# A second 7-for-8 level, in part, for the first FFN products of the last two blocks

## Chip, cores, metric

One core of a Trainium2 chip runs the whole program. The metric is device microseconds of one launch, the median of several runs. All arithmetic is in float32; the FFN weights arrive as 64-bit floats and are rounded by the kernel first.

## What is computed

```python
# attention: batch 8, heads 12, seq 448, head_dim 64
q_n, k_n = rmsnorm(q, g_q), rmsnorm(k, g_k)
attn = softmax(q_n @ k_n.T / 8)
o = attn @ v                                   # (8, 12, 448, 64)
x = o.transpose(0, 2, 1, 3).reshape(3584, 768)
# bilinear FFN: w_a, w_b are 768 x 1536, w_out is 1536 x 768
out = ((x @ w_a) * (x @ w_b)) @ w_out
```

## The kernel before, in words

**Order of the work.** Nothing is issued in the order of the source. Every step is a call `op(engine, us, key, emit, reads, writes, ...)` of a planner (`Plan`). It simulates the engines with the given costs, respects the named reads and writes and the number of buffers of each tag, and where several steps could start on an engine takes the one with the lowest key:

```python
t = min(at.values()) + (0.2 if e == "PE" else 0.05)      # line 128: how far it looks ahead
n = min((n for n in at if at[n] <= t), key=lambda n: (ops[n][2], n))
```

A step of another engine can start `LAG` = 0.1 us after what it needs. The result is one fixed order for each engine, written out at the end; the hardware then follows it, each engine strictly in its order, with semaphores where data or buffers pass between engines. Attention has keys below 24, FFN products keys from 10,000 up: matrix work of the FFN fills what attention leaves free.

**Attention.** The 96 (batch, head) pairs are taken four at a time, `p` from 0 to 23. `loads` (line 424) brings q, k, v; `normalize` squares (ACT), reduces (DVE) and takes the power -1/2 (POOL); `transposes` turns q and k on TensorE; `scores` (line 507), the exponentials on ACT, `values` (line 527) and the sums over keys follow for seven key tiles; `put_out` (line 623) copies the result into two of nine buffers of the tag `x`, and `divide` multiplies by the inverse sums. Three `p` make a batch, two batches a block; there are four blocks (`beta` 0 to 3, called blocks 1 to 4 in words).

**First FFN products.** Block `beta` holds its transposed x as four quarters B11, B21, B12, B22 (two batches by two halves of the 768 features, each 128 partitions x 3 chunks x 448 tokens). `combine` (line 653) makes three more sums T2, T3, T4 on DVE, so that a block takes seven of the nine `x` buffers. `quarter_products` (line 987) then runs, for each of 6 row groups `m` and each of the two weights, the seven products of a Strassen-Winograd scheme (seven products of half size in place of eight): each product is three matmuls of 128x128 weights by 448 tokens that add up over the three chunks. The seven weight factors were made at the start, written to DRAM (`kept`) and are streamed back by `stream` (line 406) into two buffers of the tag `st`. Each product of the second weight is multiplied into the first in `hT`, part of it on POOL.

**Last FFN products.** `last_product` (line 687) multiplies `hT` by w_out in seven products again, for tiles `t` of 128 tokens (three in an even block, four in an odd one). In blocks 3 and 4 `TWICE` (line 309) has pairs of tiles go through `inner_products` (line 859): a second level of seven products, of 128x192, with extra weight factors streamed from `kept_t` by `stream_inner` (line 846). `inner_factors` makes these during block 2.

**The order around the change.** `ffn(beta)` (line 668) is `quarter_products` for all `m`, then `last_product`. With seven of nine `x` buffers held by a block, attention can put out only one batch more until the block's first products are done; so in the trace `put_out` pauses during the first products of blocks 1, 2 and 3. The results of `p` = 21 to 23 are put out after the first products of block 3 (1137 to 1158 us), and then its last products and all of block 4 follow. `hT` has one buffer, so first products of a block wait for the last products of the block before.

## Time and profile before

| | |
|---|---|
| median of 3 runs | 1546.28 us (1545.95 to 1547.28) |
| profiled execution, first to last instruction | 1544.2 us |
| difference of the two, launch and end around the span | 2.1 us |
| TensorE clock granted | 0.999 of full |
| PE busy | 1503.3 us, 97% |
| DVE busy | 824.4 us, 53% |
| ACT busy | 401.9 us, 26% |
| POOL busy | 314.6 us, 20% |
| first products of one block alone on PE (block 4) | 189.43 us, 504 matmul instructions |

"Span" is one profiled execution; the runs are timed without a profile. A float32 matmul of the program shows as two matmul instructions (passes): the program has 12 x 7 x 3 = 252 matmuls for the first products of a block, and the chain shows 504 instructions. Each matmul instruction has a weight load (PEld) beside it. [...]what one costs in a stream is the distance from start to start. In the names of groups `pq` is a bank of the first products, `po` of the last products, `a` to `h` of `inner_products`, `sc`, `o` and `su` are attention.

### The profile page before, as it was taken

How to read it: one execution, taken by the hardware profiler on the slowest of the kernel's cores; microseconds unless marked ns; L12 is line 12 of the kernel's file. 1: busy time of each engine (PE TensorE's matmuls, PEld its weight loads, DVE VectorE, ACT ScalarE, POOL GpSimd, SP SyncE). 2: the span in 40 equal slices, each digit the busy share in tenths (PEclk: the TensorE clock that was granted, in tenths of full speed). 3: DMA queues.
4: the chain of work that ended last, by engine and by line, in shares of the span. 5: the costliest groups of instructions: out<-in, count | busy, mean ns of one | idle time of the engine just before them, and what ended most of it. 6: DMA issues, size and time to landing. Idle time of an engine off the chain costs nothing.

```text
span 1544.2 us, 18272 instructions
## 1 busy us (share of the span) xinstructions
PE 1503.3 (97%) x7068; PEld 832.2 (54%) x7068; DVE 824.4 (53%) x1215; ACT 401.9 (26%) x658; POOL 314.6 (20%) x166
## 2 busy tenths in 40 slices
PE   8988999999999999999999999999999999999998
PEld 5554345555454555555445455555546865555898
DVE  5877869888786412222587553222237622222785
ACT  6767661111567200000455500000041000000000
POOL 3417442211345200011244300000111001100100
PEclk9999999999999999999999999999999999999999
DMA  9897444544545542212345456222126752212354
GB/s 265 241 255 218 98 109 178 204 178 158 158 111 133 150 153 72 107 72 102 94 114 147 111 172 187 91 77 102 72 78 224 225 193 72 107 72 102 119 184 120
DMA packets 130019, 217.12 MB, mean 141 GB/s; under 512 B 57988, under 2 KB 108420, under 8 KB 120196
## 3 DMA queue, kind: packets, MB, share of 16 engines
q1 hardware_dynamic: 101860, 162.38, 35.9%
q10 hardware_dynamic: 28064, 53.48, 10.0%
q8 instruction: 58, 0.95, 0.3%
q14 instruction: 37, 0.30, 0.1%
HBM read 171.44 MB, written 44.21 MB: 140 GB/s over the span
## 4 chain that ended last, share of the span: by engine, by line
PE 83%; DMA 7%; ACT 3%; DVE 3%; issue 1%; POOL 1%; SPq 1%; ACTq 0%; DVEq 0%; POOLq 0%
PE pq L1003 49%; PE po L726 14%; PE sc L515 5%; PE o L537 5%; PE g L901 2%; PE a L901 2%; ACT ET L521 2%; DMA q_sb<-in_q_dram 2%; PE pt L494 2%; DMA kept_o<-st 2%; PE b L901 1%; PE su L573 1%; PE d L901 1%; PE e L901 1%; DMA k_sb<-in_k_dram 1%
## 5 line engine op out<-in xcount | busy, mean ns | idle before, releaser
L1003 PE MATMUL pq<-x,st 128*128 128x448 f32 x2016 | 763.4, 540 | 0.0
L1003 PEld LDWEIGHTS pq<-x,st 128*128 128x128 f32 x2016 | 381.2, 190 | 378.4 <-issue 370.5
L521 ACT ACTIVATE ET<-sc,ms 128x448 f32<-128x448 f32 x336 | 192.0, 635 | 92.6 <-PE sc L515 64.9
L515 PE MATMUL sc<-qkT 64*64 64x448 f32 x1344 | 177.0, 544 | 18.6 <-ACT ET L521 10.7
L537 PE MATMUL o<-ET,v_sb 64*64 64x448 f32 x1344 | 186.9, 546 | 8.0 <-ACT ET L521 7.3
L464 POOL TENSOR_TENSOR ms<-ms,expo 128x14 f32<-128x14 f32 x48 | 145.4, 3032 | 190.4 <-DVE ms L462 189.6
L1051 POOL TENSOR_TENSOR hT<-hT,t 128x448 f32<-128x448 f32 x24 | 28.5, 1186 | 743.6 <-DVE t L1049 741.3
L726 PE MATMUL po<-st,hT 128*128 128x384 f32 x432 | 142.9, 487 | 0.0
L726 PEld LDWEIGHTS po<-st,hT 128*128 128x128 f32 x432 | 81.3, 190 | 58.5 <-issue 3.4
L515 PEld LDWEIGHTS sc<-qkT 64*64 64x64 f32 x1344 | 58.7, 132 | 94.7 <-issue 32.8
L551 POOL TENSOR_TENSOR sum<-sum,ET 128x896 f32<-128x896 f32 x38 | 81.6, 2147 | 137.6 <-ACT ET L521 106.1
L1025 ACT COPY hT<-pq 128x448 f32<-128x448 f32 x24 | 12.8, 532 | 371.3 <-PE pq L1003 371.3
L537 PEld LDWEIGHTS o<-ET,v_sb 64*64 64x64 f32 x1344 | 60.3, 132 | 88.5 <-ACT ET L521 42.3
L726 PE MATMUL po<-st,fin 128*128 128x384 f32 x240 | 81.8, 491 | 0.0
L551 DVE TENSOR_TENSOR sum<-sum,ET 128x896 f32<-128x896 f32 x57 | 62.8, 1101 | 27.0 <-POOL sum L551 22.7
L1063 POOL TENSOR_TENSOR hT<-hT,t 128x448 f32<-128x448 f32 x48 | 59.0, 1231 | 53.4 <-DVE t L1060 45.2
L458 DVE TENSOR_REDUCE ms<-sq 128x14 f32<-128x896 f32 x48 | 51.8, 1079 | 28.9 <-ACT sq L456 28.9
L1056 DVE TENSOR_TENSOR hT<-U,pq 128x448 f32<-128x448 f32 x48 | 29.8, 621 | 66.2 <-PE pq L1003 66.2
L726 PEld LDWEIGHTS po<-st,fin 128*128 128x128 f32 x240 | 44.6, 190 | 35.8 <-issue 7.8
L1060 DVE TENSOR_TENSOR t<-U,pq 128x448 f32<-128x448 f32 x48 | 29.7, 619 | 58.7 <-PE pq L1003 56.6
L1028 ACT COPY t<-pq 128x448 f32<-128x448 f32 x24 | 12.8, 533 | 176.0 <-PE pq L1003 176.0
L746 DVE TENSOR_TENSOR o_sb<-fin,po 128x384 f32<-128x384 f32 x32 | 17.7, 554 | 69.2 <-PE po L726 61.5
(117 smaller groups left out, 1372.5 us busy)
## 6 DMA issues: line engine op xcount, KB each, us to landing
st<-kept SPq DMA_DIRECT2D x36, 1344.0 KB
st<-kept_o SPq DMA_DIRECT2D x28, 1152.0 KB
kept<-st ACTq DMA_DIRECT2D x12, 1344.0 KB
ti<-kept_t SPq DMA_DIRECT2D x56, 288.0 KB
q_sb<-in_q_dram SPq DMA_DIRECT2D x48, 224.0 KB
k_sb<-in_k_dram SPq DMA_DIRECT2D x48, 224.0 KB
v_sb<-in_v_dram SPq DMA_DIRECT2D x48, 224.0 KB
rec<-inv SPq DMA_DIRECT2D x48, 224.0 KB
```

Source lines behind the costliest of these rows:

```text
L458: op("DVE", 1.1, key, lambda: nc.vector.tensor_reduce(rs[p][:, s], xs["sq", nm, p], AX, ALU.add), [sq], [f"{ms}/{nm}"])
L464: lambda: nc.gpsimd.tensor_tensor(msf(), msf(), expo[:, 0:2 * NT * (b - a)], ALU.pow), [], names)
L494: nc.tensor.transpose(t[:, j * P:(j + 1) * P], x[:, j].rearrange("p h d -> p (h d)"), ident)
L515: nc.tensor.matmul(t[low_high[w], e, 0:S], lhsT=qkTs[p][low_high[e], 1, j * P + w * D:j * P + (w + 1) * D], rhs=qkTs[p][low_high[e], 0, w ...
L521: nc.scalar.activation(E[:, e], scs[p, j][:, e, 0:S], AF.Exp, scale=rs[p][:, 1, 2 * j + e:2 * j + e + 1])
L537: nc.tensor.matmul(os_[p][low_high[e], w, 0:S], lhsT=xs["v", p][low_high[w], e, j * D:(j + 1) * D], rhs=ETs[p, j][low_high[w], e], start=( ...
L551: two[e].tensor_tensor(sums[p], sums[p] if j > 1 else ETs[p, 0], ETs[p, j], ALU.add)
L726: nc.tensor.matmul(held["po"][:, 0:HALF], lhsT=a[0]()[:, c], rhs=sts[beta, 12 + place_of[f]][:, c], start=(c == 0), stop=(c == MH - 1))
L901: nc.tensor.matmul(held[bank], lhsT=x()[:, c], rhs=y(c), start=(start and c == 0), stop=(stop and c == MI - 1), skip_group_check=True)
L1003: nc.tensor.matmul(banks[bank][:, 0:S], lhsT=sts[at][:, f, c * P:(c + 1) * P], rhs=quads[x][:, c], start=(start and c == 0), stop=(stop an ...
L1056: take("DVE", 0.68, lambda bank=bank, i=i, n=n: V.tensor_tensor(C(i, n), held["U"], PS(bank), ALU.add), [f"p{ident_}.{bank}", U], [hp[i]])
L1063: lambda i=i, n=n, nm=nm: two[TIMES].tensor_tensor(C(i, n), C(i, n), held[nm], ALU.mult), [t], [hp[i]],
```

## The change

1. Blocks 3 and 4 (`DEEP`) no longer use `quarter_products`. `deep_products` takes the two weights together: for each `m` and each of the seven factors `f` it forms a two-by-two product (two weights by two chunks of the sum, two halves of 224 tokens) with one more seven-for-eight level over chunks 1 and 2 of 3, and plainly adds the third chunk. A step (m, f) has 11 matmuls of 224 tokens; its part of the work before was 12 of that size. There are 42 steps in a block.
2. The extra weight factors are made during the first products of block 2 (`PREP`) by `deep_factors` (5 DVE steps on 896 elements and 5 DRAM writes of 448 KB for each m) and streamed back with the old ones, three transfers of 640 KB together for each step, into quarters of the two `st` buffers. The token sums (4 DVE steps for each of 7 quarters) sit in buffers of attention (`ET`, `sum`, `rec`, `qn`).
3. The products leave PSUM into seven buffers F (tags `q`, `k`, `v`, `sq`), are combined there by DVE (`wide`), and multiplied by POOL into `hT` (`times`).
4. In the plan, attention from `p` = 15 on is loaded after the first products of block 2, all attention ends before the deep products of block 3, and T2 and T4 of block 3 are made after it, in `qkT` buffers, so that nine `x` buffers do.
5. In blocks 3 and 4 the last product f = 0 is a plain one (`TWICE` without 0), split in halves over the sum, the first of which need only the first three `m`.

The diff, cut to its core:

```diff
-        TWICE = {NB - 2: (0, 1, 2, 3, 4, 5, 6), NB - 1: (0, 1, 2, 3, 4, 5, 6)}
+        TWICE = {NB - 2: (1, 2, 3, 4, 5, 6), NB - 1: (1, 2, 3, 4, 5, 6)}
         MAKE = 1
         ONCE = NB - 2
+        DEEP, PREP = (NB - 2, NB - 1), NB - 3
+        HELD = 2 * HC * (PREP + 1) + HC * (XS - 7) // 2
...
-            op("SP", 0.8 if nm != "k" else 1.4, p - (1.8 if nm == "v" else 2.0), emit, [], [t], new=[t],
+            op("SP", 0.8 if nm != "k" else 1.4, p - (1.8 if nm == "v" else 2.0), emit, [f"firsts{PREP}"] if p >= HELD else [], [t], new=[t],
...
-        def combine(beta, c):
+        def combine(beta, c, part=None):
             B11, B21, B12, B22, T2, T3, T4 = names_of(beta)
-            for to, x, y in ((T3, B22, B12), (B12, B12, B11), (T2, B22, B12), (T4, B21, T2)):
+            steps = ((T3, B22, B12), (B12, B12, B11), (T2, B22, B12), (T4, B21, T2))
+            for to, x, y in steps if part is None else steps[2 * part:2 * part + 2]:
                 first = c == 0 and to != B12
-
-                def emit(to=to, x=x, y=y, first=first):
+                tag, bufs = ("qkT", 2) if part else ("x", XS)
+                def emit(to=to, x=x, y=y, first=first, tag=tag, bufs=bufs):
                     if first:
-                        quads[to] = wk.tile([P, KH, S], FP32, tag="x", name="x", bufs=XS)
+                        quads[to] = wk.tile([P, KH, S], FP32, tag=tag, name="x", bufs=bufs)
                     nc.vector.tensor_tensor(quads[to][:, c], quads[x][:, c], quads[y][:, c], ALU.subtract)
                 if first:
-                    tile_of(to, "x", XS)
-                op("DVE", 0.63, -0.5, emit, [f"{x}/{c}", f"{y}/{c}"], [f"{to}/{c}"] + (["quarter"] if first else []),
-                   new=[to] if first else [], lock=True)
-
-        def ffn(beta):
-            B11, B21, B12, B22, T2, T3, T4 = names_of(beta)
+                    tile_of(to, tag, bufs)
+                op("DVE", 0.63, -0.5, emit, [f"{x}/{c}", f"{y}/{c}"] + ["ended"] * bool(part),
+                   [f"{to}/{c}"] + (["quarter"] if first and not part else []), new=[to] if first else [], lock=True)
+        def firsts(beta):
+            names = names_of(beta)
             key = 1e4 + beta * 1e3
...
-            op(None, 0.0, 0, open_h, [], [f"{h}/{m}" for m in range(KO)], new=[h])
+            op(None, 0.0, 0, open_h, [], [f"{h}/{m}" for m in range(KO)] + [f"{h}/open"], new=[h])
+            if beta in DEEP:
+                deep_products(beta, key, names, h)
+                return
             for n, (m, ab) in enumerate(order):
                 if beta:
                     stream(beta, n)
                     st, at = f"st{beta}.{n}", (beta, n)
                 else:
                     st, at = f"st{n}", n
-                quarter_products(beta, key, m, ab, st, at, (B11, B21, B12, B22, T2, T3, T4), h)
-            last_product(beta, h, key + 100)
+                quarter_products(beta, key, m, ab, st, at, names, h)
+                if beta == PREP and ab:
+                    deep_factors(beta, m)
+        def lasts(beta):
+            last_product(beta, f"h{beta}", 1e4 + beta * 1e3 + 100)
...
+        def deep_factors(beta, m):
+            st, ts = [f"st{beta}.{2 * m + ab}/0" for ab in range(2)], {}
+            w = lambda ab, c: (lambda: sts[beta, 2 * m + ab][:, :, c * P:(c + 1) * P])
+            made = lambda n: (lambda: ts[n])
...
+            for n, x, y, alu, reads in ((0, w(1, 0), w(1, 1), ALU.add, []), (1, made(0), w(0, 0), ALU.subtract, [0]),
+                                        (2, w(0, 0), w(1, 0), ALU.subtract, []), (3, w(0, 1), made(1), ALU.subtract, [1]),
+                                        (4, w(0, 2), w(1, 2), ALU.subtract, [])):
+                nm = tile_of(f"dk{m}.{n}", "ET", 4)
+                def emit(n=n, x=x, y=y, alu=alu):
+                    ts[n] = wk.tile([P, 2, S], FP32, tag="ET", name="ds", bufs=4).rearrange("p a b -> p (a b)").rearrange(
+                        "p (f n) -> p f n", f=7)
+                    nc.vector.tensor_tensor(ts[n], x(), y(), alu)
+                op("DVE", 1.05, -0.5, emit, st + [f"dk{m}.{x}" for x in reads], [nm, "deep factors"], new=[nm], lock=True)
+                op("SP", 0.5, 0, lambda n=n: nc.sync.dma_start(kept["s"][:, m, :, n], ts[n]), [nm], [f"ks{m}.{n}"], kb=448)
+        def deep_products(beta, key, names, h):
+            B11, B21, B12, B22, T2, T3, T4 = names
...
+            sums_of = {}
+            for f, x in enumerate(xs_of):
...
+                nm = sums_of[f] = tile_of(f"dT{beta}.{f}", tag, bufs)
+                block = lambda n, f=f: deep["T", f][:, n * HS:(n + 1) * HS]
+                token = lambda k, n, x=x: quads[x][:, k, n * HS:(n + 1) * HS]
+                for n, a, b in ((0, lambda t=token: t(0, 1), lambda t=token: t(0, 0)), (1, lambda t=token: t(1, 1), lambda k=block: k(0)),
+                                (2, lambda t=token: t(1, 1), lambda t=token: t(0, 1)), (3, lambda t=token: t(1, 0), lambda k=block: k(1))):
+                    def emit(n=n, a=a, b=b, tag=tag, bufs=bufs, f=f, block=block):
...
+                        V.tensor_tensor(block(n), a(), b(), ALU.subtract)
+                    op("DVE", 0.32, -0.4, emit, [f"{x}/0", f"{x}/1", "ended" if beta == ONCE else f"{h}/open"] + ([nm] if n else []),
+                       [nm], new=[] if n else [nm], lock=True)
...
+            def step(m, f, F, names_F):
+                C = lambda i, n: hTs[0][:, m + MH * i, n]
+                at, turn = (7 * m + f) % 4, (7 * m + f) % 3
+                slot = f"{homes[at // 2]}/{at % 2}"
+                W = lambda n, k=1: deep["st", at // 2][:, (at % 2) * KH * P * 7 // 2 + n * P:][:, 0:k * P]
+                def load():
+                    nc.sync.dma_start(W(0, 3), kept[2 * m][:, f * KH * P:(f + 1) * KH * P])
+                    nc.sync.dma_start(W(3, 2), kept[2 * m + 1][:, f * KH * P + P:(f + 1) * KH * P])
+                    nc.sync.dma_start(W(5, 5), kept["s"][:, m, f].rearrange("p n c -> p (n c)"))
+                op("SP", 0.9, 6.0 * beta + (7 * m + f) / 14, load, [f"kept{2 * m}", f"kept{2 * m + 1}"] + [f"ks{m}.{n}" for n in range(5)],
+                   [slot], kb=655, dmas=3)
+                id_, held = f"{beta}.{m}.{f}", {}
+                home = ("o", 1) if turn == 1 else ("sc", 2)
+                a_, sc_ = tile_of(f"da{id_}", "mm", 2), tile_of(f"dg{id_}", *home)
+                gb, gg = f"{sc_}/0", f"{sc_}/1"
+                x, T = xs_of[f], sums_of[f]
+                B = lambda k, n: (lambda: quads[x][:, k, n * HS:(n + 1) * HS])
+                Tn = lambda n: (lambda: deep["T", f][:, n * HS:(n + 1) * HS])
+                def product(nm, to, terms, reads, new=None, more=False):
+                    def emit():
+                        if new == a_:
+                            held["a"] = ps_mm.tile([P, 512], FP32, tag="mm", name="da")
+                        elif new:
+                            held["g"] = (ps_o if turn == 1 else ps_s).tile([P, 2, 512], FP32, tag=home[0], name="dg")
+                        for k, (w, t) in enumerate(terms):
+                            nc.tensor.matmul(to(), lhsT=W(w), rhs=t(), start=not more and k == 0, stop=k == len(terms) - 1,
+                                             skip_group_check=True)
+                    op("PE", len(terms) * HS / 595, key + 0.1 * (7 * m + f), emit, reads + [slot], [nm, "ffn"],
+                       new=[new] if new else [], mode="full")
+                a = lambda: held["a"][:, 0:HS]
+                bank = lambda n, c: (lambda: held["g"][:, n, c * HS:(c + 1) * HS])
+                tt = tile_of(f"dt{id_}", "t", 2)
+                part = lambda n: held["t"][:, n * HS:(n + 1) * HS]
...
+                Ft = names_F[f] = tile_of(f"dF{id_}", tag, bufs)
+                def copy():
+                    held["t"] = wk.tile([P, S], FP32, tag="t", name="dt", bufs=2)
+                    nc.scalar.copy(part(0), a())
+                def first():
...
+                    F[f] = t.rearrange("p a b c -> p (a b c)" if tag == "k" else "p a b -> p (a b)")
+                    nc.scalar.copy(F[f][:, 0:HS], a())
+                allF = lambda g: [f"{names_F[g]}/{n}" for n in range(3)]
+                def wide(to, other):
+                    take("DVE", 1.02, lambda: V.tensor_tensor(F[to], F[to], F[other], ALU.add), allF(other), allF(to), lock=True)
+                def times(g, i, n):
+                    e = "DVE" if m == MH - 1 and f > 4 else TIMES
+                    take(e, 1.2 if e == "POOL" else 0.63,
+                         lambda: two[e].tensor_tensor(C(i, n), F[g][:, 0:S], F[g][:, S:2 * S], ALU.mult), allF(g),
+                         [f"{h}/{m + MH * i}"], lock=True)
+                halves = lambda t: t.rearrange("p (n s) -> p n s", n=2)
+                rest_of_a = lambda: product(a_, a, [(1, B(1, 0)), (2, B(2, 0))], [f"{x}/1", f"{x}/2"], more=True)
+                product(a_, a, [(0, B(0, 0))], [f"{x}/0"], new=a_)
+                take("ACT", 0.35, copy, [a_], [tt], [tt])
+                if m == f == 0:
+                    rest_of_a()
+                product(gb, bank(0, 0), [(6, Tn(1))], [T], new=sc_)
+                product(gb, bank(0, 1), [(7, Tn(2))], [T])
+                take("DVE", 0.38, lambda: V.tensor_tensor(part(1), part(0), bank(0, 0)(), ALU.add), [gb, tt], [tt])
+                take("DVE", 0.38, lambda: V.tensor_tensor(part(0), part(1), bank(0, 1)(), ALU.add), [gb, tt], [tt])
+                if m or f:
+                    rest_of_a()
+                take("ACT", 0.35, first, [a_], [f"{Ft}/0"] + ([f"firsts{beta}"] if (m, f) == (MH - 1, 6) else []), [Ft])
+                yield
+                product(gg, bank(1, 0), [(3, Tn(3)), (4, B(2, 0))], [T, f"{x}/2"])
+                product(gg, bank(1, 1), [(5, Tn(0)), (4, B(2, 1))], [T, f"{x}/2"])
+                take("DVE", 0.66, lambda: V.tensor_tensor(
+                    halves(F[f][:, S:2 * S]), part(0).rearrange("p (o s) -> p o s", o=1).to_broadcast([P, 2, HS]),
+                    halves(held["g"][:, 1, 0:S]), ALU.add), [gg, tt], [f"{Ft}/1"])
+                yield
+                product(gg, bank(1, 1), [(8, B(1, 1)), (9, B(2, 1))], [f"{x}/1", f"{x}/2"], more=True)
+                take("DVE", 0.38, lambda: V.tensor_tensor(F[f][:, HS:S], part(1), bank(1, 1)(), ALU.add), [gg, tt], [f"{Ft}/2"])
+                if f == 1:
+                    wide(1, 0)
+                    times(1, 0, 0)
+                elif f == 2:
+                    wide(2, 0)
+                elif f in (3, 4):
+                    wide(f, 2)
+                elif f == 5:
+                    wide(3, 5)
+                    wide(5, 4)
+                    times(5, 1, 1)
+                    times(3, 1, 0)
+                elif f == 6:
+                    wide(6, 4)
+                    times(6, 0, 1)
+                yield
+            before = None
+            for m in range(MH):
+                F, names_F = {}, {}
+                for f in range(7):
+                    now = step(m, f, F, names_F)
+                    next(now)
+                    if before:
+                        next(before)
+                    next(now)
+                    before = now
+            ends[beta] = before
...
+                begun = {}
                 for t in pairs if not twice else alone:
-                    product(t, f, a(t), plain(t, base, to))
+                    begun[t] = product(t, f, a(t), plain(t, base, to))
+                if f == 0 and beta in ends:
+                    next(begun[0])
+                    next(ends[beta])
+                    next(begun[1])
+                    yield
+                    for t in pairs[:2]:
+                        next(begun.pop(t))
+                else:
+                    yield
+                for x in begun.values():
+                    next(x)
+                    next(x)
                 for g in twice:
                     inner_products(beta, key + place_of[f], f, g, a, base, to, acc, (c_, U_), out_place)
...
-                    combine((p - 1) // (2 * HC), 0)
+                    combine((p - 1) // (2 * HC), 0, part)
                 if p % (2 * HC) == 0:
-                    combine(p // (2 * HC) - 1, 1)
-                    combine(p // (2 * HC) - 1, 2)
+                    combine(p // (2 * HC) - 1, 1, part)
+                    combine(p // (2 * HC) - 1, 2, part)
                     if p // (2 * HC) <= ONCE:
-                        ffn(p // (2 * HC) - 1)
+                        firsts(p // (2 * HC) - 1)
+                        lasts(p // (2 * HC) - 1)
                     elif p == NC:
-                        for beta in range(ONCE, NB):
-                            ffn(beta)
+                        for c in range(KH):
+                            combine(ONCE, c, 1)
+                        firsts(ONCE)
+                        lasts(ONCE)
+                        firsts(NB - 1)
+                        lasts(NB - 1)
```

## Prediction

> **What bounds the kernel now.** I read the page first, then the groups by form, the stages (busy time by window), the chain of work that ended last, and the timeline of a few microseconds.
>
> ```profile
> PE 1503.3 (97%) x7068; PEld 832.2 (54%) x7068; DVE 824.4 (53%) x1215; ACT 401.9 (26%) x658; POOL 314.6 (20%) x166
> PE 83%; DMA 7%; ACT 3%; DVE 3%; issue 1%; POOL 1%; SPq 1%; ACTq 0%; DVEq 0%; POOLq 0%
> ```
>
> TensorE (PE) is busy throughout and is 83% of the chain.
>
> ```profile
> 571.20:747.00 175.80, 175.80 (x469) 88.92 (x468) 37.84 (x61) 9.05 (x17) 16.96 (x15) 1.00 0.25 89
> 747.00:884.00 137.00, 132.35 (x938) 60.47 (x937) 98.23 (x125) 79.65 (x134) 60.63 (x25) 1.00 0.47 123
> 961.50:1137.00 175.50, 175.50 (x468) 88.72 (x467) 43.42 (x71) 9.05 (x17) 16.97 (x15) 1.00 0.25 89
> 1171.00:1248.50 77.50, 76.67 (x379) 63.47 (x378) 52.83 (x109) 4.64 (x11) 1.38 (x1) 1.00 0.75 244
> 1248.50:1437.80 189.30, 189.30 (x506) 95.64 (x505) 49.27 (x87) 9.58 (x18) 19.47 (x17) 1.00 0.26 90
> ```
>
> Columns: window, length, busy PE, PEld, DVE, ACT, POOL with counts, clock, DMA share, GB/s. The first products (rows 1, 3, 5) have PE without a gap, DVE at a quarter, DMA at a quarter: only fewer PE cycles shorten them, and there is room for more DVE and DMA work.
>
> ```profile
> 961.47 178.14 PE pq L1003 x474
> 1248.52 189.43 PE pq L1003 x504
> 1502.53 1.18 PE g L901 x6
> 1509.57 1.18 PE g L901 x6
> ```
>
> In the chain, block 4's first products are one link: 189.43 / 504 = 375.9 ns a pass, no handoff visible. The second level that exists already (L901) differs: one link breaks out of each group, 7.04 us apart. A group is 42 passes of 128x192, from start to start 162.4 ns (0.974 us for six), so 6.82 us: 0.21 us is lost in each. The timeline shows where:
>
> ```profile
> 1487.33 1.14 PE L901 MATMUL e<-st,Si 128*128 128x192 f32 x6
> 1488.00 0.35 DVE L957 TENSOR_TENSOR fin<-pi,g 128x192 f32<-128x192 f32 x1
> 1488.41 0.95 PEld L901 LDWEIGHTS g<-ti,fin 128*128 128x128 f32 x6 [0.23 <-DVE fin L957]
> 1488.41 1.24 PE L901 MATMUL g<-ti,fin 128*128 128x192 f32 x6
> 1489.49 1.14 PE L901 MATMUL a<-st,fin 128*128 128x192 f32 x6
> ```
>
> PE could go on at 1487.33 + 0.974 = 1488.30. It adds to bank `g`, which DVE still reads until 1488.35; the weight load starts 0.06 later, and six passes then take 1489.49 - 1488.41 = 1.08, that is 0.106 over 0.974. Lost: 0.21. So a bank coming back from DVE costs 0.06 + 0.106 after DVE ends. In the other direction, a bank's last pass ends its slot at 1443.20 and DVE starts at 1443.40: 0.20.
>
> **The Trainium skill.** "TensorE: Matmul & The Clock Gate", Back-to-back issue gap, has N/2.4 + 2.5 ns. The trace agrees if a float32 pass counts its columns twice: 162.4 at 192, 375.9 at 448. "VectorE: DVE Perf Modes", The TRN2 errata, gives (N + 151)/0.96 ns for a float32 tensor_tensor: 357 at 192, 1091 at 896; the trace has 357 and 1089 to 1101. "PSUM — Partial Sum Buffer", PSUM bank collisions, wants two engines kept apart by bank, not by address: hence PE waits for DVE above, and will in the new steps. "Perfetto Trace Analysis", Tensor Engine Instruction, calls a matmul's end an estimate; I therefore count from start to start.
>
> **The change, part by part.**
>
> *Matmuls.* A 224-column pass, on the line through 162.4 and 375.9, is 189.1 ns. That weight loads (190 ns in the record) don't stop it is shown by 162.4 at 192. For each m: before 84 x 375.9 = 31.58 us; after 7 x 11 x 2 x 189.1 = 29.12. Twelve m: **-29.4 us**, all on the path.
>
> *Handoffs inside a step.* PE's order follows from the plan: it looks 0.2 us ahead and takes the lowest key. In a step, counted from its start: a (1 matmul), gb, gb, the two further of a, then four of gg; the last two (weights 8, 9) of the step before have the lower key. They add into the bank of gg that DVE must read first (128x448, 0.62 us as in L1060). In the plan's costs that is ready at 0.10 + 0.66 + 0.10 = 0.86, and at 0.75 PE is free: within 0.2, so they go third, after a and gb. On the chip: DVE starts at 0.20, ends 0.82, weights at 0.88, stream again at 0.98, while PE was free at 0.757: **0.22 us lost**. Where DVE does two 896-wide sums first (after f = 5) the pair goes later and nothing is lost: six of seven steps, 72 in all, **+16.1**. The other return, ACT's copy of `a`, fits: first pass pair over at 0.378, ACT 0.20 later for 0.35 (between 0.32 at 192 and 0.53 at 448), back at about 0.98, needed by 1.9. DVE per m: 7 x (3 x 0.39 + 0.62) + 7 x 1.09 = 20 of 30 us, room enough. Bounds: 0 if DVE's work falls elsewhere, 0.5 a step if it is late as well.
>
> *Factors.* 30 DVE sums of 1.09 in block 2's first products: 37.8 + 33 of 175.8 us of DVE. Hidden by PE; in block 1 the same products stream at 376 with DVE busy 17 to 18 of 20 us. Writes of 13.4 MB on SP's queue lie among loads that come every 16 us. Nothing; if uncovered, a few tenths per sum.
>
> *Streams.* 655 KB in 4.2 us is 157 GB/s, three issues of 0.32 us on SP. The stage at 1171 moved 244 GB/s. Hidden, four slots ahead.
>
> *Attention moved.* Pairs from p = 15 load after block 2's first products; SP has only stores and loads of the last products behind those loads. Nine pairs then meet block 2's last products alone (336 passes of 322.5 = 108 us). At 747 to 884 six pairs used 48 us of FFN work as filler; nine need some 72, and about 15 us pass before the first pair is ready: enough. Pairs in that stretch take 14.9 us of PE each, those at 140 to 220, with little filler, 16.2. I take **+1.5**; bounds -2 (one restart of attention fewer) and +12 (no filler, 9 x 1.3).
>
> *Ends of first products.* Last products need every m. At the last step DVE has two sums, two multiplies and the bank read; then the pair 8, 9, one add, one sum, one multiply before the second half of f = 0 may start. PE has two half products (2 x 1.94) to cover; by the same counting 2.3 us stay open for each block, against 0.3 at 1439 now: **+4**.
>
> *Starts.* Block 4's token sums wait for the last products' DVE work, and `a` is completed ahead of gb: about 2 us; block 3's are ready, 0.5. **+2.5**. T2 and T4 in DVE's slack: nothing.
>
> *f = 0 plain.* A group costs 7.04 now, two plain tiles 24 x 322.5 = 7.74: +0.7 for three groups, 2.1; but DVE is at 17.8 of 20 us there and stalls PE (1.8 us at 1481): I take **0**, bounds -3 and +2.8. Its factors load later; f = 0 covers them: **+0.5**.
>
> Sum: -29.4 + 16.1 + 1.5 + 4 + 2.5 + 0.5 = -4.8. Against the execution's own 1544.2: 1539.4; the 2.1 us around it, which bring it to the median of 1546.28, stay: **1541.5**.
>
> **Rivals.** (B) The bank reads find other matmuls to hide behind: -29.4 + 8.5 + 4 = -17, 1529. For it: first products now lose nothing. Against: L901's groups lose 0.21 each. (C) Slower: the handoff in each step is longer, DVE's backlog of wide sums reaching the bank read of gg. The other terms leave 20.9 us over 84 steps, so from 0.25 us a step the gain is gone; at 0.45, 37.8 - 20.9 = +17, 1563. For it: one order on DVE, 20 us per m of work. Against: no step but the sixth has two sums. (D) Attention runs out of filler, or token sums come late: +10 on the forecast, 1551. For it: p = 15 starts cold. Against: the count of 72 of 108. (E) That 224-column passes don't reach 189 ns is excluded by 162.4 at 192.
>
> **How the numbers follow.** Forecast 0.45, spread about ±5: two thirds of it faster by over 0.2% (3.1 us, about what a measurement of this kernel can tell from no change), one third within. B 0.20, faster. C 0.20, slower. D 0.15: slower but for 0.03 within. Faster 0.30 + 0.20 = 0.50, within 0.15 + 0.03 = 0.18, slower 0.32. Between 1528 and 1558 lies all but C's worse half and a part of B. Both signs hold chance; the forecast alone spans 1536 to 1547.
>
> **What would show it.** Steps of the new line at about 4.38 us, 4.16 where two sums precede; weight loads of the pair 8, 9 released by DVE, some 70 times; first products of blocks 3 and 4 at 183 us each in place of 189.4; PE idle of about 2 us where they end. Wrong if a step is steadily under 4.25 or over 4.6, or if PE stands more than 10 us between the last products of block 2 and the deep steps.

## The result, and the profile after

| | before | after |
|---|---|---|
| median of 4 runs each, same chip | 1546.12 us (1545.09 to 1547.28) | 1519.41 us (1517.36 to 1524.65) |
| ratio, 95% interval | | 0.9838 [0.9815, 0.9861] |
| profiled execution, span | 1544.2 us | 1515.7 us |
| PE busy, matmul instructions | 1503.3 us, 7068 | 1477.4 us, 7854 |
| DVE busy | 824.4 us | 1009.6 us |

Faster by 1.6%; the prediction had 1541.5, and 1528 as its lower end. The page after, busy times first, then the chain that ended last by engine:

```profile
PE 1477.4 (97%) x7854; PEld 981.6 (65%) x7854; DVE 1009.6 (67%) x1568; ACT 441.2 (29%) x790; POOL 324.7 (21%) x172
...
PE 86%; DMA 6%; DVE 3%; ACT 2%; issue 1%; SPq 1%; ACTq 0%; DVEq 0%
```

PE still bounds the kernel and DVE's share of the chain has not grown, though it works 185 us more. The stages, in the columns explained with the prediction (block 2's first products with the new factors; the deep products of block 3, of block 4):

```profile
541.60:731.00 189.40, 189.40 (x505) 95.99 (x505) 73.24 (x100) 9.58 (x18) 19.21 (x17) 1.00 0.53 163
...
972.40:1153.30 180.90, 178.30 (x930) 173.59 (x929) 130.94 (x233) 28.61 (x84) 23.91 (x21) 1.00 0.54 162
1228.90:1409.30 180.40, 177.99 (x931) 173.80 (x930) 135.41 (x259) 28.56 (x84) 23.66 (x21) 1.00 0.55 163
```

Row 1: the factors cost PE nothing, it is busy for all of its 189.40 us, with DVE at 73 us. Rows 2 and 3: 924 deep passes and 6 or 7 of the last products in 181 us; of that PE stands idle for 2.5 us. The chain through two deep steps (start, length, link):

```profile
1092.52 2.40 PE dg L779 x12
...
1096.81 2.27 PE dg L779 x12
1099.08 0.38 PE da L779 x2
1099.46 0.76 PE dg L779 x4
1100.21 0.76 PE da L779 x4
1100.97 2.27 PE dg L779 x12
```

From 2.27 to 2.27 are 4.16 us: 22 passes of 189.1 ns and nothing else. Only where two wide sums precede, in ten steps, is a link 2.40 us long, 0.13 more (first line). The chain also gives the order of PE: after `a` (2 passes) and gb (4) come the two further matmuls of `a` (4), and only then the pair with weights 8 and 9 of the step before, ahead of gg (12 = 4 + 8). The prediction had the pair third. The timeline shows why that matters:

```profile
1103.28 0.62 DVE L826 TENSOR_TENSOR dF<-dt,dg 128x448 f32<-128x448 f32 x1
1103.45 0.92 PE L779 MATMUL dg<-dT,st 128*128 128x224 f32 x4
...
1104.21 0.92 PE L779 MATMUL da<-x,st 128*128 128x224 f32 x4
...
1104.97 0.35 PE L779 MATMUL dg<-x,st 128*128 128x224 f32 x1
```

DVE's read of gg's bank (L826) lasts from 1103.28 to 1103.90; the pair that adds into that bank comes at 1104.97, a microsecond later. What PE waits for on line 779, from the list of waits (total, times, longest):

```profile
PE dg L779 <- DVE dF L826: 2.0, 2, 1.0
PE dg L779 <- DVE dt L819: 1.9, 2, 1.0
PE da L779 <- ACT dt L792: 1.1, 3, 0.4
```

Two, two and three waits, all at the first and last steps of the two blocks. In between nothing shows in this list; there is only the 0.13 us of the ten longer links.

**A caution on spans.** Up to the end of block 1's first products both kernels do the same, yet the profiled executions end that stage at 424.2 and 420.7 us, and the kernels below at 419.8 to 425.1; the changed kernel itself, profiled a second time, at 424.2. So up to 5 us of a difference of two spans may be chance; I compare stages within a trace and medians of runs.

### The profile page after: what moved, and what is told of

The parts are those of the page before. It is cut to its first block, busy times and chain, and to the rows that moved or that the text cites. A ratio compares the mean times of both kernels' runs of the same rounds, so it can differ in the third digit from the quotient of the medians.

```text
span 1515.7 us, 21017 instructions
## 1 busy us (share of the span) xinstructions
PE 1477.4 (97%) x7854; PEld 981.6 (65%) x7854; DVE 1009.6 (67%) x1568; ACT 441.2 (29%) x790; POOL 324.7 (21%) x172
## 4 chain that ended last, share of the span: by engine, by line
PE 86%; DMA 6%; DVE 3%; ACT 2%; issue 1%; SPq 1%; ACTq 0%; DVEq 0%
PE pq L1202 25%; PE dg L779 17%; PE po L903 15%; PE da L779 6%; PE o L539 6%; PE sc L517 6%; PE g L1100 2%; PE a L1100 2%; PE pt L496 2%; DMA q_sb<-in_q_dram 2%; PE su L575 1%; ACT ET L523 1%; PE b L1100 1%; DMA kept_o<-st 1%; PE d L1100 1%
## 5 line engine op out<-in xcount | busy, mean ns | idle before, releaser
L1202 PE MATMUL pq<-x,st 128*128 128x448 f32 x1008 | 382.4, 541 | 0.0
L1202 PEld LDWEIGHTS pq<-x,st 128*128 128x128 f32 x1008 | 190.8, 190 | 188.7 <-issue 181.7
L779 PE MATMUL dg<-x,st 128*128 128x224 f32 x672 | 169.6, 355 | 2.0 <-DVE dF L826 2.0
L779 PE MATMUL dg<-dT,st 128*128 128x224 f32 x672 | 168.3, 353 | 1.9 <-DVE dt L819 1.9
L807 POOL TENSOR_TENSOR hT<-dF 128x448 f32<-128x448 f32 x42 | 47.6, 1143 | 427.3 <-DVE dF L802 427.3
L779 PEld LDWEIGHTS dg<-x,st 128*128 128x128 f32 x672 | 126.5, 190 | 5.3 <-DVE dF L826 5.3
L779 PEld LDWEIGHTS dg<-dT,st 128*128 128x128 f32 x672 | 126.7, 190 | 3.2 <-DVE dt L819 2.8
L779 PE MATMUL da<-x,st 128*128 128x224 f32 x504 | 123.2, 353 | 1.1 <-ACT dt L792 1.1
L779 PEld LDWEIGHTS da<-x,st 128*128 128x128 f32 x504 | 93.0, 190 | 4.5 <-ACT dt L792 2.1
L802 DVE TENSOR_TENSOR dF<-dF 128x896 f32<-128x896 f32 x84 | 93.3, 1111 | 3.4 <-DVE dF L831 0.5
```

The source lines that it names most:

```text
L779: nc.tensor.matmul(to(), lhsT=W(w), rhs=t(), start=not more and k == 0, stop=k == len(terms) - 1, skip_group_check=True)
L802: take("DVE", 1.02, lambda: V.tensor_tensor(F[to], F[to], F[other], ALU.add), allF(other), allF(to), lock=True)
L807: lambda: two[e].tensor_tensor(C(i, n), F[g][:, 0:S], F[g][:, S:2 * S], ALU.mult), allF(g),
L1202: nc.tensor.matmul(banks[bank][:, 0:S], lhsT=sts[at][:, f, c * P:(c + 1) * P], rhs=quads[x][:, c], start=(start and c == 0), stop=(stop an ...
```

## The experiments

The kernel before was run beside each; ratios are to it.

| kernel | median us | ratio, 95% interval |
|---|---|---|
| e1, pair third, by hand | 1623.73 | 1.0518 [1.0502, 1.0534] |
| e2, order of the attention alone | 1552.24 | 1.0051 [1.0037, 1.0064] |
| e3, deep products in block 4 alone | 1534.38 | 0.9926 [0.9912, 0.9939] |
| e4, f = 0 plain alone | 1548.85 | 1.0025 [1.0015, 1.0034] |
| e7, order and f = 0 plain | 1543.67 | 0.9997 [0.9989, 1.0005] |
| the changed kernel again | 1520.88 | 0.9839 [0.9824, 0.9854] |
| e5, pair fourth | 1517.01 | 0.9831 [0.9814, 0.9847] |
| e9, products not chained | 1564.99 | 1.0128 [1.0112, 1.0144] |
| e11, as e9, gb and gg in two tiles | 1527.88 | 0.9896 [0.9880, 0.9913] |
| e8, edges of the blocks | 1517.55 | 0.9824 [0.9808, 0.9840] |
| e12, as e8, gb and gg in two tiles | 1512.92 | 0.9801 [0.9787, 0.9816] |

### Which part brings the gain

**e4: the kernel before, f = 0 plain.**

```diff
-TWICE = {NB - 2: (0, 1, 2, 3, 4, 5, 6), NB - 1: (0, 1, 2, 3, 4, 5, 6)}
+TWICE = {NB - 2: (1, 2, 3, 4, 5, 6), NB - 1: (1, 2, 3, 4, 5, 6)}
```

> The kernel before with one edit: f = 0 of the last products of blocks 3 and 4 plain, not by the second level (TWICE without 0). Theory 1 (three groups of 7.04 us become six tiles of 3.87): 2 us over the kernel before, 1548. Rival 1 (the prediction's term: the relief of DVE pays for it): no change, 1546. Rival 2: 3 us under it, 1543.

Measured +4.0, by the interval 2.3 to 5.3: a cost, where the prediction had nothing and a bound of 2.8. In the two traces each of blocks 3 and 4 is 1.3 us longer, 2.6 together; another 2.7 us lie behind the last matmul, at the very end (see "Open").

**e2: the changed kernel's order of attention, with the first and last products of before.**

```diff
-TWICE = {NB - 2: (1, 2, 3, 4, 5, 6), NB - 1: (1, 2, 3, 4, 5, 6)}
+TWICE = {NB - 2: (0, 1, 2, 3, 4, 5, 6), NB - 1: (0, 1, 2, 3, 4, 5, 6)}
-DEEP, PREP = (NB - 2, NB - 1), NB - 3
+DEEP, PREP = (), NB - 3
-                if beta == PREP and ab:
+                if DEEP and beta == PREP and ab:
```

> The changed kernel's order of attention alone: all of attention ends before block 3, T2 and T4 of block 3 in qkT buffers, but the first products of blocks 3 and 4 as before (quarter_products), f = 0 of the last products as before, no extra factors. Theory 1 (fewer interruptions of attention are worth what the two traces differ by between the first products of block 1 and the start of block 3): 4 to 6 us under the kernel before, 1540 to 1542. Rival (the prediction's term): 0 to 2 us over it, 1546 to 1548; then the deep steps alone brought all of the gain.

Both theories missed: +7.3. By stages, the time from the end of block 1's first products to the end of block 3's is 3.9 us shorter (742.6 for 746.5), but after block 4's first products 9.7 us more pass to the end. The chain there:

```profile
1431.93 2.65 PE pq L1202 x7
...
1435.44 6.03 DMA ti<-kept_t
```

The weight factors of the first two-level group (`ti`) are loaded only after the first products end; nothing covers them, and PE stands for 6 us. The kernel before has loaded them before these first products begin, 190 us earlier:

```profile
1243.86 2.62 SPq L856 DMA_DIRECT2D ti<-kept_t  x3
...
1248.75 2.01 SPq L856 DMA_DIRECT2D ti<-kept_t  x1
```

This is not the order of the attention, which is over long before block 4 in both kernels. The change also makes `stream_inner` wait for the end of its block's first products, because the buffers of the tags `q`, `k`, `v` and `ET` that it loads into hold F and the token sums until then, and e2 has kept that condition though it has no deep products:

```diff
-                op("SP", 0.5, 6.0 * beta + (12 + place_of[f]) / 4, load, [f"kt{f}.{n}.0", f"kt{f}.{n}.{MI - 1}", "ended"], [nm], new=[nm], kb=295)
+                op("SP", 0.5, 6.0 * beta + (12 + place_of[f]) / 4, load, [f"kt{f}.{n}.0", f"kt{f}.{n}.{MI - 1}", "ended", f"firsts{beta}"], [nm], new=[nm], kb=295)
```

So e2 is not the order alone, and its 6 us say nothing against the order. e3 below shows the same: its block 3 has first products and f = 0 as in the kernel before, with attention running between them, but also this condition, and PE waits there too:

```profile
1172.65 2.19 PE L1100 MATMUL b<-ti,Si 128*128 128x192 f32 x6 [3.05 <-DMA ti<-kept_t]
```

In e2, in the 20 us from the end of block 4's first products on, PE is busy 13.53 us, at a granted clock of 0.83 (the third number from the end, ahead of DMA share and GB/s):

```profile
1434.40:1454.00 19.60, 13.53 (x75) 13.26 (x74) 13.51 (x27) 1.28 (x4) 1.40 (x2) 0.83 0.56 198
```

**e7: order and f = 0 plain together**, e2 without its first two diff lines; the condition on `stream_inner` is in it too.

> The order of the attention of the change, and f = 0 plain in the last products of blocks 3 and 4, but the first products as before (12 matmuls, no deep factors). The order alone, with f = 0 at two levels, gave 1552.2; f = 0 plain alone gave 1548.9; the kernel before has 1544.9. Theory (the 6 us wait for the factors of block 4's f = 0 in the run with the order alone, and the slower clock after it, come from loads that may start only when the first products end; plain f = 0 has no such loads, so the two edits need each other): the attention is 3.9 us shorter, f = 0 plain costs 2.1 to 4.0 us, nothing waits: 1543 to 1546, the same as before. Rival (the costs add: +7.3 and +4.0): 1554 to 1557.

Measured 1543.67: no different from before. The same stretch of its trace has no gap:

```profile
1430.00:1450.00 20.00, 20.00 (x77) 13.61 (x76) 11.10 (x21) 2.24 (x5) 1.13 (x1) 1.00 0.65 236
```

So plain f = 0 belongs with the deep products: they keep the factors from being loaded early, and it is the work that covers the late load. The order without that condition was not run by itself. Both edits together give nothing, and the gain comes with the deep products: 1543.67 to 1520.88, corrected for the two runs of the kernel before (1544.15 and 1544.71), is -23.3 us.

**e3: deep products in block 4 alone**, with the order of attention of before around block 3; the loads from `p` = 15 on stay held until block 2's first products end. f = 0 has two levels again in block 3.

```diff
-TWICE = {NB - 2: (1, 2, 3, 4, 5, 6), NB - 1: (1, 2, 3, 4, 5, 6)}
+TWICE = {NB - 2: (0, 1, 2, 3, 4, 5, 6), NB - 1: (1, 2, 3, 4, 5, 6)}
-DEEP, PREP = (NB - 2, NB - 1), NB - 3
+DEEP, PREP = (NB - 1,), NB - 3
...
-                part = 0 if (p - 1) // (2 * HC) == ONCE else None
+                part = None
...
-                        for c in range(KH):
-                            combine(ONCE, c, 1)
```

> Deep products and plain f = 0 in block 4 alone; block 3 has its first products and its attention order as before (pairs 21 to 23 after the first products of block 3). Pairs from 15 on still load after the first products of block 2, where the extra factors are made. Theory 1 (a deep step costs its 22 passes of 189 ns and nothing more, the ends of the block some 5 to 6 us): 9 us under the kernel before, 1537. Rival (a handoff of 0.22 us in each step, as predicted): 1 us under it, 1545.

Measured -10.5: one block brings close to half of the gain, though block 3 stands 3 us for its factors.

### Where the pair stands

**e1: the pair third.** My theory after the result was that the order had saved the handoff. This kernel sets the pair by hand where the prediction had it: a, one gb, the pair.

```diff
                 product(gb, bank(0, 0), [(6, Tn(1))], [T], new=sc_)
+                yield
...
                     if before:
                         next(before)
                     next(now)
+                    next(now)
```

> The changed kernel with one edit: in every deep step the two matmuls that complete the step before (weights 8 and 9) are issued third, after a and one gb, where the prediction believed them to be, and not after the two further matmuls of a. Theory 1 (the arithmetic of a bank that comes back from DVE was right, only its place in PE's order was wrong, because all FFN products are chained in the order of the source by the name ffn): 0.22 us lost in most of the 84 steps, and 0.6 to 0.8 in the twelve behind two wide sums, so 16 to 25 us over the changed kernel: 1536 to 1545. Rival (PE takes such a return without loss at this size): at most 4 us over it, under 1524.

Measured +79 beside the kernel before, 104 over the changed kernel: far beyond both. The pair loses what the arithmetic says (PE free at 1153.33, streaming again at 1153.56 in its trace), but a second wait appears which neither theory had:

```profile
1149.38 1.09 DVE L802 TENSOR_TENSOR dF<-dF 128x896 f32<-128x896 f32 x1
...
1150.20 0.54 PE L779 MATMUL dg<-x,st 128*128 128x224 f32 x2
...
1151.28 0.39 DVE L820 TENSOR_TENSOR dt<-dt,dg 128x224 f32<-128x224 f32 x1
...
1151.72 0.65 PE L779 MATMUL dg<-dT,st 128*128 128x224 f32 x2 [0.97 <-DVE dt L820]
```

The wide sum (L802) goes ahead of the two adds of gb; gg's first product is then issued ahead of the adds, the adds wait for it, and gg's second product waits 0.97 us for the adds. That happens 66 times, and such a step lasts 5.63 us in place of 4.16.

**e5: the pair fourth**, after both gb, ahead of `a`'s two further matmuls: the `yield` stands ahead of `if m or f: rest_of_a()` instead.

> Theory (the place of the pair decides, and the border lies between the third and the fourth place): the only edit moves the pair of matmuls with weights 8 and 9 of the step before from behind a's two further matmuls to ahead of them, so one matmul later than in the kernel with the pair third. There the tensor engine was free 0.757 us after the end of gg and the bank came back about 0.22 us later; in the fourth place it is free at 4 x 0.378 = 1.135 us less the start of the count, 0.15 us after the bank is back (0.98). So nothing waits for the bank, and the adds have the pair and a's matmuls (1.51 us) ahead of gg as before: 1517 to 1522, the same as the changed kernel within 3 us. Rival (it is not the place, but any order in which the pair and the adds meet on the vector engine costs, as the 1.2 us a step of the kernel with the pair third suggests): over 1530, with gg's second product waiting for the adds about 60 times.

Measured 1517.01 beside 1520.88, with ranges that overlap (1515.91 to 1520.86, 1517.84 to 1521.95): the same. One matmul of 0.378 us between the third place and the fourth decides whether the handoff is seen.

**e9: the chain taken away.** Why does the plan put the pair last? Every FFN product names `"ffn"` among what it writes, so each depends on the one before it in the source. For matrix work of the FFN the lookahead has nothing to choose from.

```diff
-                    op("PE", len(terms) * HS / 595, key + 0.1 * (7 * m + f), emit, reads + [slot], [nm, "ffn"],
+                    op("PE", len(terms) * HS / 595, key + 0.1 * (7 * m + f), emit, reads + [slot], [nm] + ["ffn"] * (new == a_),
```

> The edit takes the shared name that chains all FFN products in source order from the deep products other than a's first; nothing else is changed. Theory (my step failed because the chain fixes the order of the tensor engine, not because the planner's 0.2 us lookahead works otherwise): without the chain the planner puts the pair third, as the prediction had it, with the adds ahead of the wide sums, so the pair waits about 0.22 us in each of some 82 steps, +18 us; and gg, which the order of emission holds for the adds of its own step with only a's two matmuls (0.757 us) between, may wait up to 0.35 us a step more. 1537 to 1566; the prediction's 1541.5 is the lower half of that. Rival (the wait of the pair goes with the wide sums and the adds, and alone it is absorbed): 1518 to 1525.

Measured 1564.99, the upper end. In its trace the pair is third:

```profile
1100.48 0.62 DVE L826 TENSOR_TENSOR dF<-dt,dg 128x448 f32<-128x448 f32 x1 [0.87 <-PE dg L779]
1100.66 0.54 PE L779 MATMUL dg<-dT,st 128*128 128x224 f32 x2
...
1101.16 1.02 PE L779 MATMUL dg<-x,st 128*128 128x224 f32 x4
...
1102.40 0.92 PE L779 MATMUL da<-x,st 128*128 128x224 f32 x4
...
1103.09 0.39 DVE L819 TENSOR_TENSOR dt<-dt,dg 128x224 f32<-128x224 f32 x1
...
1103.53 0.65 PE L779 MATMUL dg<-dT,st 128*128 128x224 f32 x2 [0.21 <-DVE dt L819]
```

gb's two passes are over at 1100.66 + 2 x 0.189 = 1101.04; DVE has read the bank at 1101.10; the pair's stream begins at 1101.16 + 0.106 = 1101.27: 0.23 lost. `a` is over at 1102.40 + 4 x 0.189 = 1103.16, and gg streams at 1103.53 + 0.106 = 1103.64: 0.48 more. The list of waits has both, 66 times:

```profile
PEld dg L779 <- DVE dt L819: 41.8, 66, 1.3
...
PEld dg L779 <- DVE dF L826: 20.7, 66, 1.0
```

Counted from start to start over all steps, gg loses 0.48 us in 53 steps, 0.74 in 12 and 1.22 at the start of each block, 37 in all, and the pair about 15. In the 12 steps the second add first waits for gg's first product, as in e1. The deep products take 205.7 and 204.8 us against 180.9 and 180.3 in the unchanged kernel beside it, 49 together; 4 of these are twelve more passes of last products that fall into the two stretches. The other 45 fit the medians, which differ by 44 us.

**e11: the same order, two tiles.** gg writes bank 1 of its tile, the adds read bank 0, and gg's operands are token sums and weights. Nothing but the tile is shared. In e11 gb and gg of a step lie in two tiles; the order on every engine is that of e9.

```diff
-                home = ("o", 1) if turn == 1 else ("sc", 2)
-                a_, sc_ = tile_of(f"da{id_}", "mm", 2), tile_of(f"dg{id_}", *home)
-                gb, gg = f"{sc_}/0", f"{sc_}/1"
+                homes_of = [("o", 1) if (turn + y) % 3 == 1 else ("sc", 2) for y in range(2)]
+                a_, sc_, gg_ = tile_of(f"da{id_}", "mm", 2), tile_of(f"db{id_}", *homes_of[0]), tile_of(f"dg{id_}", *homes_of[1])
+                gb, gg = f"{sc_}/0", f"{gg_}/1"
...
```

> The kernel without the chain (1565.0) once more, with the same order on every engine; only gb and gg of a step now lie in two PSUM tiles instead of the two halves of one. Theory (gg waits for the adds of its own step only because both use one tile: it writes another bank and reads nothing that the adds write): the wait of gg, 0.48 us in 66 steps, 31.7 us, goes altogether; the wait of the pair for its bank, 0.226 us in as many steps and a little more, stays: 1532 to 1538, still 12 to 18 above the changed kernel. Rival (gg waits for the bank as such, or for the vector engine for another reason): 1560 to 1566.

Measured 1527.88, 37 below e9 and 4 below the expected range; deep products at 186.3 and 186.8 us, 37 less as well. The wait of the pair is still there, that of gg is not:

```profile
1103.23 0.68 PEld L780 LDWEIGHTS dg<-x,st 128*128 128x128 f32 x4 [0.31 <-DVE dF L827]
...
1104.47 0.92 PE L780 MATMUL da<-x,st 128*128 128x224 f32 x4
...
1105.16 0.39 DVE L820 TENSOR_TENSOR dt<-dt,db 128x224 f32<-128x224 f32 x1
1105.22 0.54 PE L780 MATMUL dg<-dT,st 128*128 128x224 f32 x2
```

gg starts at 1105.22, with no wait, while the second add (1105.16 to 1105.55) is still reading. So the wait was the program's, not the chip's. It fits the Trainium skill, "PSUM — Partial Sum Buffer", PSUM bank collisions raise a hardware error: two engines on different banks run clean. The 37 us are the whole of what gg lost in e9; the expectation had counted 0.48 in all of the 66 steps, 32, and so left out the longer waits of 12 steps and of the two starts.

### The edges of the blocks

In the changed kernel these are the waits at the start of block 3 and at its end:

```profile
973.36 1.02 PE L779 MATMUL da<-x,st 128*128 128x224 f32 x4 [0.43 <-ACT dt L792]
...
976.86 0.65 PE L779 MATMUL dg<-dT,st 128*128 128x224 f32 x2 [0.96 <-DVE dt L819]
...
1152.63 1.02 PE L779 MATMUL dg<-x,st 128*128 128x224 f32 x4 [1.01 <-DVE dF L826]
```

The first step has `a`'s rest ahead of gb, where it waits 0.43 us for ACT, and then nothing stands between gb's adds and gg, in the same tile. In the last step DVE does two wide sums and two multiplies before it reads gg's bank (from 1151.97), and six passes of the plain f = 0 (1.9 us) are all that stands between gg and its pair.

**e8** moves `a`'s rest: behind gb in the first step of block 3, behind gg in the last step of both blocks.

```diff
-                if m == f == 0:
+                closing, early = (m, f) == (MH - 1, 6), m == f == 0 and beta != ONCE
+                if early:
                     rest_of_a()
...
+                if closing:
+                    rest_of_a()
+                    take("ACT", 0.35, lambda: nc.scalar.copy(F[f][:, 0:HS], a()), [a_], [f"{Ft}/0", f"firsts{beta}"])
                 yield
                 product(gg, bank(1, 1), [(8, B(1, 1)), (9, B(2, 1))], [f"{x}/1", f"{x}/2"], more=True)
```

> Two edits at the edges of the deep blocks. The first step of block 3 has a's two further matmuls behind gb, as all other steps have, where the changed kernel has them ahead of gb (block 4 stays, its token sums come late); and the last step of each block has them behind gg instead of ahead of it, so that 0.757 us of matmuls stand between gg and the pair that waits for its bank. Theory (the idle times of the trace there, 0.43 + 0.96 us at the start of block 3 and 1.01 us at each end, are waits that other matmuls can cover): -1.4 us and twice -0.75 us, 1516.5 where the changed kernel has 1519.4, a ratio of 0.998 between the two. Rival (what is late next, the sums of the last step on the vector engine, takes it back): 1518.5 to 1520.5.

> The changed kernel once more, unchanged, beside the three kernels below. Expected 1517 to 1521 (1519.4 so far, 0.984 of the kernel before). It is the measure for the other three, so that none of them is compared across chips.

The medians differ by 3.3 us with overlapping ranges. By stages, block 3 from its first deep matmul to that of block 4 takes 254.7 us for 256.5, block 4 to the end 285.9 for 286.4: -2.3, where -2.9 was expected.

**e12** adds the two tiles of e11 to e8, so that gg does not wait at the starts either.

> The kernel with the two edits at the edges, with gb and gg in two tiles as well. Theory: inside the blocks nothing waits, so nothing changes there; at the start of block 4 gg's wait for the adds (0.97 us), and at that of block 3 its rest (0.20 us, some 0.3 with the weights), go: -1.2 us against 1517.5, 1515.5 to 1517.5, to be read from the stages more than from the median. Rival (a tile that now has two users in turn comes free later, and gb of a later step waits for it): over 1519, with waits of gb for the last add of a step.

Measured 1512.92 beside 1544.86: below the expected range, and faster than the changed kernel, whose interval in the second comparison lies above (0.9787 to 0.9816 against 0.9824 to 0.9854; the first comparison's begins at 0.9815). By stages it is -0.6 (block 3) and -1.4 (block 4 to the end) against e8, -2.0 where -1.2 was expected. Its deep products:

```profile
971.50:1150.00 178.50, 177.64 (x930) 173.96 (x929) 130.77 (x233) 28.64 (x84) 23.90 (x21) 1.00 0.54 161
1225.60:1404.00 178.40, 177.68 (x931) 174.01 (x930) 135.11 (x259) 28.66 (x84) 23.63 (x21) 1.00 0.54 160
```

PE idles 0.9 and 0.7 us in each block, where it idled 2.6 and 2.4. It is the fastest version measured here.

## Why the prediction was wrong

**Matmuls, -29.4: right.** A pass takes 2.27 / 12 = 0.189 us, and most steps have no other cost.

**Handoffs inside a step, +16.1: the step that failed.** Its sentence "at 0.75 PE is free: within 0.2, so they go third" applied the rule of the lookahead to products that are not free to be chosen: all are chained by the name `"ffn"` in the writes of `product`. The pair is issued after `a`'s two further matmuls, at 1.89 by the prediction's own clock, and the bank is back at 0.98. In place of 0.22 in 72 steps there is 0.13 us after each pair of wide sums, ten times, and 0.08 once: about +1.4. Steps at 4.16 us, under 4.25, are also what the prediction had named as a sign of being wrong. So where the prediction had nothing lost, there is a little, and where it had the loss, there is none. The price itself was right: where the pair does stand third (e9, e11), the trace has 0.23 a step in 66 steps. What the prediction did not have is what else comes with that order: 0.48 us a step and more for gg, because of a shared tile. With its order in this program the time is 1565, not 1541.5 (e9); with the order and separate tiles it is 1527.9 (e11). So rival B came nearest for the reason it named, other matmuls behind which the bank reads hide. Rival C, the slower one, is what e9 shows, with another cause than DVE's backlog.

**Order of attention +1.5, f = 0 plain 0: each wrong, their sum nearly right.** f = 0 costs 4.0 by the medians (e4), 2.6 in its two stages, where the prediction's own arithmetic had 2.1; the relief of DVE, for which it took the 2.1 away, does not show. The order brings about as much (e7 minus e4, and 3.9 in the stages of e2); together -0.5 [-1.7, +0.8]. That plain f = 0 covers its late factors was right: without it PE stands for 6 us (e2), with it there is no gap (e7), so the +0.5 set aside for it is not there.

**Ends +4 and starts +2.5: right in sum, not in place.** From e7 to the changed kernel, block 3 from its first pass to that of block 4 shrinks by 10.3 us (266.8 to 256.5) and block 4 from there to the last matmul by 10.7 (290.8 to 280.1), 21.0; against 29.4 that leaves 8.4. Counted from start to start, the trace has 1.4 inside the steps, 1.9 at each start, 1.3 at each end, and 0.5 in block 3's last step, where `a` waits for ACT: 8.3, of which 6.9 are edges. (The idle times in brackets above are shorter, 1.4 at a start and 1.0 at an end: they begin at a matmul's recorded end, which lies 0.16 us behind its slot, and leave out the 0.106 until the stream runs again.) Block 3's start costs as much as block 4's, which the prediction denied: the wait is not for token sums, but for ACT and for the adds of a shared tile.

**Factors and streams, 0: right.** Block 2's first products take 189.40 us with PE busy throughout, and DMA moves 162 GB/s in the deep stage without a wait of PE for `st`.

The sum of the misses: handoffs 16.1 - 1.4 = 14.7; order, f = 0 plain and its factors 1.5 + 0.5 + 0.5 = 2.5; edges 6.5 - 6.9 = -0.4. Together 16.8, so -4.8 becomes -21.6. The second comparison measured -23.8 (1544.71 to 1520.88). The 2 us between them are about what e7's trace has more than the changed kernel's behind the last matmul (8.6 against 6.3 and 6.7), so they are no work of the deep products that I can name. The first comparison, -26.7, lies 3 lower; its interval takes in -23.8.

**Open.** Why attention in one piece is shorter by some 4 us was not tested by itself. e2, e4 and e7 take 8.6 to 9.0 us from the start of their last matmul to the end, the other kernels 6.3 to 7.1. That is 2.7 us of e4's difference from the kernel before and 2 us of what the deep products seem to bring over e7. Each is read from one profile, and the cause was not found.

## What to carry to other kernels

Before a rule of a scheduler is used to say where an instruction goes, look whether its dependencies leave it a choice; one name written by all may fix the whole order. A bank that comes back from DVE cost 0.2 us here where it was needed at once, and nothing one matmul of 0.378 us later (e5), so count the matmuls between. And a semaphore wait can come from a shared tile alone: if neither bank nor data is shared, give the two their own tiles before moving work around. When one part of a change is taken out to be measured alone, look for the conditions that belong to it: e2 kept one, and so measured something else than the order that it was to test.

## What the runs showed of the hardware

Weight loads of 190 ns in the record did not hold back passes of 189.1 ns, 42 steps long, with PEld busy 174 of 181 us. DVE added a 128x224 bank in 0.386 us; the Trainium skill, "VectorE: DVE Perf Modes", The TRN2 errata, gives (224 + 151) / 0.96 = 391 ns, and the trace agrees within 1.3%. A stall of PE of 6 us (e2) went with a granted clock of 0.83 over the 20 us around it; in the same stage without the stall it stayed at 1.00 (e7). Once PE ran again, the clock was 0.59 for the first 3.4 us and 1.00 from then on. After the stall of 3.05 us in e3 it was 0.55 for 3.8 us; after one of 2.03 us in e2's block 3 it stayed at 1.00.
